# Last FFN's weights loaded early in 128-row chunks, V buffers shared, and a planner that prices waiting

## Chip, cores, metric

One core of a Trainium2 chip. The metric is the device time of one execution in microseconds (us). Executions of one kernel scatter by 4 to 20 us here, so kernels are compared by ratios of runs on the same chip. Profiles are single executions. In them PE is TensorE, PEld its weight loads, DVE VectorE, ACT ScalarE, POOL GpSimd, and SP SyncE, which issues the loads of weights (SPq is its queue). "issue" is a wait for nothing that the profile shows. Buffer numbers are left out, so W is both the Q and K weights and the small buffer of w1 and w3. A step is one segment of each layer at work, and a pair of an FFN is 256 of its 4608 hidden columns, gate and up.

## The reference, cut to what matters

```python
x = A_x                                    # 2048 x 576
x = x + _A_ref(_layernorm(x), ...)         # recurrent memory attention, 64 segments of 32 rows
x = x + _B_ref(_layernorm(x), ...)         # gated FFN, 576 -> 4608 -> 576
x = x + _A_ref(_layernorm(x), ...)         # the same weights again
x = x + _B_ref(_layernorm(x), ...)
# in _A_ref, for each segment s: h = [mem (8 rows), xs (32 rows)]; q, k, v = h Wq, h Wk, h Wv
# (32 heads of 128); o = softmax(q k / sqrt(128) + mask) v Wo; mem = o[:8]; out = o[8:]
```

The memory makes the 64 segments of one attention layer a chain. The kernel runs layer 2 eight segments behind layer 1: steps 0 to 7 have one layer, 8 to 63 two, 64 to 71 one. Every four steps a block of 128 rows is ready for an FFN, whose work fills TensorE between the parts of the chain. The last FFN, after step 71, has nothing beside it.

## The kernel before

A planner in Python simulates the engines and fixes the order of all work. On TensorE it takes, of the items that can start first, the one of lowest priority number plus a penalty if it needs another tiling mode (full, 64-row, 32-column, ...):

```python
if e == "PE":
    key = lambda x: x[1].prio + (mode_pen if x[1].mode != mode else 0.0)
...
pool_ = [x for x in ests if x[0] <= t + 1e-9]
pick = min(pool_, key=key)
```

V products of a segment come in two pieces (one in one-layer steps), each with its own buffer; a tail of 64 rows in another mode follows each piece:

```python
for k in ((0,) if one else (0, 1)):
    sl = Slot(f"vx{k}", users=4 if one else 2)
    m_ = node("PE", 8 * 0.2165, em.vx(t, k, b, False),
              deps=deps + [vx_pe.get(k), vx_pe.get(1) if one else None], ..., mode="c32", acq=[sl] + b)
    n = vx_pe[k] = node("PE", 0.2165, em.vx(t, k, b, True), deps=[m_], ..., mode="oct")
```

The FFNs stream their weights through small buffers. The last one loads them, in nine chunks, over the attention weights (W for Q and K, WV, WO), when all that reads the last segment is done, in halves of 64 rows:

```python
tail = [load("tail", kb(128, 9 * 512 + 4 * 576), s0 + 0.01 * i, em.tail_load(i),
             deps=reads_ht[nst - 1] + ([yx[1, nseg - 1]] if i == 8 else [])) for i in range(9)]
...
for r, wd in ((0, self.a.w1), (R64, self.a.w3)):      # tail_load
    self.dma(t13[r:r + R64], wd[:, fa:fa + 512].rearrange("(c p) f -> p c f", p=R64))
...
for fb in range(2):                                    # ffn_up: 36 matmuls of 64 rows per pair
    for c in range(NCH):
        for r in (0, 1):
            rr = slice(r * R64, (r + 1) * R64)
            self.mm(self.bk(b[r])[...], W[rr, c, fb * P:(fb + 1) * P], self.T.XTB[rr, POS[c], lo:hi], ...)
```

## Time and profile before

| | before |
|---|---|
| median | 2974.65 us (2973.45 to 2979.82, 4 runs) |
| TensorE busy | 96% |
| from the rows of step 63 to those of step 70 (one-layer steps) | 235.7 us |
| from the rows of step 70 to the last instruction | 109.8 us |

"The rows of step k" is, here and below, the moment at which ScalarE starts to copy step k's memory rows from PSUM into HT; it ends one step of the chain, and the timeline shows it. The prediction shows the main lines. Three further rows of the busy times by stretch (start:end, length, busy of PE, PEld, DVE, ACT, POOL with instructions, clock, DMA share, GB/s) cut the end as the result needs it:

```profile
2631.40:2867.10 235.70, 228.83 (x6248) 188.36 (x6245) 169.37 (x419) 88.62 (x255) 4.24 (x7) 1.00 0.54 124
2867.10:2908.60 41.50, 30.57 (x824) 24.59 (x816) 20.19 (x53) 11.40 (x34) 0.58 (x1) 0.90 0.72 158
2908.60:2976.90 68.30, 41.22 (x731) 33.13 (x730) 25.10 (x60) 10.48 (x24) 1.15 (x2) 0.75 0.91 180
```

One-layer steps with PE busy 97%; step 71, 41.5 us; the last FFN and the store, 68.3 us with PE busy 60% and DMA at 0.91.

### The profile page before, as it was taken

How to read it: one execution, taken by the hardware profiler on the slowest of the kernel's cores; microseconds unless marked ns; L12 is line 12 of the kernel's file. 1: busy time of each engine (PE TensorE's matmuls, PEld its weight loads, DVE VectorE, ACT ScalarE, POOL GpSimd, SP SyncE). 2: the span in 40 equal slices, each digit the busy share in tenths (PEclk: the TensorE clock that was granted, in tenths of full speed). 3: DMA queues.
4: the chain of work that ended last, by engine and by line, in shares of the span. 5: the costliest groups of instructions: out<-in, count | busy, mean ns of one | idle time of the engine just before them, and what ended most of it. 6: DMA issues, size and time to landing. Idle time of an engine off the chain costs nothing.

```text
span 2976.9 us, 147413 instructions
## 1 busy us (share of the span) xinstructions
PE 2866.2 (96%) x68021; PEld 2342.9 (79%) x68021; DVE 2068.5 (69%) x5015; ACT 1078.2 (36%) x2684; POOL 63.7 (2%) x108
## 2 busy tenths in 40 slices
PE   5999999999999999999999999999999999999985
PEld 4777878788888888888888888888888888888874
DVE  3566677776767777776777677677867777677753
ACT  1343333333334333343434333333433334333431
POOL 0000000000000000000000000000000000000000
PEclk7999999999999999999999999999999999999997
DMA  9065544444444444435344543444444444545479
GB/s 291 4 134 121 118 105 105 100 96 98 98 106 99 98 97 105 103 88 114 90 103 92 116 100 90 99 104 98 97 99 104 100 98 93 117 101 122 114 156 185
DMA packets 483275, 324.46 MB, mean 109 GB/s; under 512 B 16600, under 2 KB 477792, under 8 KB 482656
## 3 DMA queue, kind: packets, MB, share of 16 engines
q1 hardware_dynamic: 479584, 307.96, 45.9%
q8 instruction: 531, 8.70, 1.3%
q0 software_dynamic: 3072, 7.08, 0.8%
q14 instruction: 88, 0.72, 0.1%
HBM read 310.26 MB, written 2.36 MB: 105 GB/s over the span
## 4 chain that ended last, share of the span: by engine, by line
PE 90%; issue 3%; DMA 3%; DVE 2%; ACT 1%; SPq 1%; POOLq 0%; POOL 0%; DVEq 0%; ACTq 0%
PE bank L478 70%; PE YB L478 13%; PE SB L478 7%; DMA W<-in_B_w_dram 1%; DMA W<-in_A_Wk_dram 1%; ACT HT L481 1%; SPq L487 1%; DVE QKT L484 1%; DVE SME L484 0%; DVE STAT L484 0%; ACT QKT L481 0%; DVE PB L484 0%; DVE HT L484 0%; DVE HTT L484 0%; ACT XTB L481 0%
## 5 line engine op out<-in xcount | busy, mean ns | idle before, releaser
L478 PEld LDWEIGHTS <-W 128*128 128x128 bf16 (+1 forms) x34632 | 1241.4, 97 | 163.3 <-issue 71.2
L478 PE MATMUL bank<-HT,W 128*128 128x80 bf16 (+3 forms) x23040 | 807.6, 197 | 13.9 <-issue 5.5
L478 PE MATMUL bank<-XTB,W 64*128 64x256 bf16 (+1 forms) x11592 | 621.4, 260 | 21.4 <-DMA W<-in_B_w_dram 10.9
L481 ACT ACTIVATE QKT<-bank 128x320 bf16<-128x320 f32 (+1 forms) x801 | 279.7, 408 | 591.7 <-PE bank L478 589.2
L478 PE MATMUL bank<-WV,HT 128*32 128x512 bf16 (+3 forms) x8000 | 457.8, 386 | 11.2 <-DMA WV<-in_A_Wv_dram 5.4
L478 PE MATMUL YB<-OT,WO 128*128 128x80 bf16 (+1 forms) x11520 | 436.4, 197 | 15.3 <-issue 8.2
L478 PEld LDWEIGHTS <-WO 128*128 128x128 bf16 x11520 | 411.2, 99 | 44.1 <-issue 32.4
L481 ACT ACTIVATE HTT<-bank 128x512 bf16<-128x512 f32 (+1 forms) x324 | 178.1, 550 | 434.9 <-PE bank L478 432.7
L478 PEld LDWEIGHTS <-HT 128*32 128x32 bf16 (+3 forms) x8000 | 174.2, 93 | 201.7 <-issue 53.8
L484 DVE TENSOR_TENSOR PB<-SME,STAT 40x256 bf16<-40x256 f32 (+1 forms) x1024 | 320.4, 318 | 17.2
L478 PE MATMUL bank<-W2C,HTT 128*128 128x288 bf16 x2232 | 321.8, 287 | 0.6 <-DVE HTT L484 0.2
L484 DVE TENSOR_REDUCE STAT<-SME 104x8 f32<-104x320 f32 (+1 forms) x576 | 276.9, 481 | 55.8 <-ACT SME L481 48.7
L484 DVE SCALAR_TENSOR_TENSOR XR<-bank,XR 128x288 f32<-128x288 f32 x576 | 246.9, 450 | 68.6 <-PE bank L478 61.7
L484 DVE SCALAR_TENSOR_TENSOR HTT<-HTT,bank 128x512 bf16<-128x512 bf16 (+1 forms) x324 | 202.1, 624 | 126.1 <-ACT HTT L481 122.0
L478 PEld LDWEIGHTS <-HTT 128*128 128x128 bf16 x2304 | 205.1, 98 | 61.8 <-DVE HTT L484 7.2
L481 ACT ACTIVATE OT<-bank 128x320 bf16<-128x320 f32 (+1 forms) x356 | 137.5, 408 | 298.9 <-PE bank L478 294.3
L484 DVE CAST QKT<-bank 128x320 bf16<-128x320 f32 (+1 forms) x351 | 144.3, 446 | 145.9 <-PE bank L478 145.2
L484 DVE TENSOR_TENSOR HTT<-HTT,bank 128x512 bf16<-128x512 bf16 (+1 forms) x324 | 203.6, 628 | 24.5 <-DVE HTT L484 0.5
L484 DVE TENSOR_TENSOR SME<-SB,maskb 104x320 f32<-104x320 f32 (+1 forms) x288 | 136.8, 475 | 85.1 <-PE SB L478 81.2
L484 DVE CAST VX<-bank 128x512 bf16<-128x512 f32 x127 | 83.8, 686 | 156.4 <-PE bank L478 156.3
L481 ACT ACTIVATE SME<-SME 104x320 f32<-104x320 f32 (+1 forms) x288 | 135.2, 469 | 152.9 <-DVE SME L484 152.2
L484 DVE CAST OT<-bank 128x320 bf16<-128x320 f32 (+1 forms) x220 | 97.8, 446 | 109.1 <-PE bank L478 107.1
(63 smaller groups left out, 1922.0 us busy)
## 6 DMA issues: line engine op xcount, KB each, us to landing
W<-in_B_w_dram SPq DMA_DIRECT2D x612, 288.0 KB, 4.9
W2C<-in_B_w_dram SPq DMA_DIRECT2D x306, 288.0 KB, 4.0
W<-in_B_w_dram SPq DMA_DIRECT2D x16, 576.0 KB, 15.2
XR<-in_A_x_dram POOLq DMA_DIRECT2D x16, 288.0 KB, 3.0
WO<-in_A_Wo_dram SPq DMA_DIRECT2D x4, 1152.0 KB, 8.6
WV<-in_B_w_dram SPq DMA_DIRECT2D x8, 576.0 KB, 15.5
W<-in_A_Wq_dram SPq DMA_DIRECT2D x8, 512.0 KB, 8.1
W<-in_A_Wk_dram SPq DMA_DIRECT2D x8, 512.0 KB, 9.1
```

Source lines behind the costliest of these rows:

```text
L478: self.ch("PE", self.nc.tensor.matmul(out, lhsT=lhsT, rhs=rhs, start=start, stop=stop, skip_group_check=True, **k))
L481: self.ch("ACT", self.nc.scalar.activation(*a, **k))
L484: self.ch("DVE", getattr(self.nc.vector, fn_)(*a, **k))
L487: self.ch("SP", self.nc.sync.dma_start(out=out, in_=in_))
```

## The change

Its intent: the loads for the last FFN start as soon as the weights that they overwrite are dead (V weights after the last V product, then W, then WO); 128-row chunks; job 16, the last but one FFN, spreads over 3.0 steps for 3.64; V buffers go to whichever piece is next, and each piece waits for the tail of the piece before it (the chain); the planner looks 16 ns ahead, prices waiting, and gives a bonus to modes with much ready work; the priorities are tuned anew. Cut to its core:

```diff
-        key = lambda x: x[1].prio + (mode_pen if x[1].mode != mode else 0.0)
+        pool_ = [x for x in ests if x[0] <= t + o.hor]
+        work = {}
+        for x in pool_:
+            work[x[1].mode] = work.get(x[1].mode, 0.0) + x[1].dur
+        key = lambda x: (x[1].prio + o.wait * (x[0] - t)
+                         + (o.mode_pen - o.bulk * min(work[x[1].mode], 4.0) if x[1].mode != mode else 0.0))
...
-    qk, qkt, sc, ... = 0.0372, -0.0358, 0.0268, ...        # 15 of 17 priorities differ
+    qk, qkt, sc, ... = 0.0079, -0.0342, 0.0268, ...
+    ... hor, wait, bulk, ff_split, last_win, tail_at = ..., 0.0162, 0.141, 0.02, False, 3.0, -1.5
...
-            sl = Slot(f"vx{k}", users=4 if one else 2)
+            sl = Slot("vx", users=4 if one else 2)
-            m_ = node(..., deps=deps + [vx_pe.get(k), vx_pe.get(1) if one else None], ...)
-            n = vx_pe[k] = node(...)
+            m_ = node(..., deps=deps + [vx_pe.get(0)], ...)
+            n = ... = vx_pe[0] = node(...)
...
+        if t == nst - 1:                     # step 71: V of the memory rows first
+            m_.prio = n.prio = t
+            last_reads[0].extend([m_, n])
...
-            tail = [load(..., deps=reads_ht[nst - 1] + ...) for i in range(9)]
+                    parts = [(None, 9 * 512 + 4 * 576, v_done if i < 2 else qk_done if i < 8 else o_done)]
+                tail.append([load("tail", ..., s0 + o.tail_at + 0.01 * i, em.tail_load(i, what), deps=dep) ...])
-                prio = s0 + o.ff + o.win * pr_ / NPR
+                prio = s0 + o.ff + (o.win if s0 + 4 < nst else o.last_win) * pr_ / NPR
...
+                for kind, wd in ((0, self.a.w1), (1, self.a.w3)):          # tail_load, 128 rows
+                    self.dma(t13[:, 4 * kind:4 * kind + 4], wd[0:4 * P, fa:fa + 512].rearrange("(c p) f -> p c f", p=P))
+                if tail is False:                                          # ffn_up: 16 full + 4 half
+                    for r in (0, 1):
+                        for c in range(4):
+                            self.mm(self.bk(b[r])[:, os_], W[:, 4 * r + c, fs], self.T.XTB[:, c, lo:hi], ...)
```

More of the change, by code (lines that the diff above doesn't have):

```diff
@@ L37 @@
 POS = [c // 2 if c % 2 == 0 else 4 + c // 2 for c in range(NCH - 1)] + [8]
-POOLS = {"bank": 6, "s": 1, "y": 1, "qkt": 4, "vx0": 1, "vx1": 1, "vm": 1, "sme": 2, "pb0": 1, "pb1": 1, "pts": 1, "ot": 1,
+POOLS = {"bank": 6, "s": 1, "y": 1, "qkt": 4, "vx": 2, "vm": 1, "sme": 2, "pb0": 1, "pb1": 1, "pts": 1, "ot": 1,
          "xr": 4, "xn": 2, "w13": 2, "w2": 3, "htt": 4}
@@ L65, in after, with plan @@
         self.left = len(self.deps)
-def plan(nodes, pools, mode_pen=0.12, hold=0.0):
+def plan(nodes, pools, o):
     for n in nodes:
@@ L114, in plan @@
         if e == "PE":
-            key = lambda x: x[1].prio + (mode_pen if x[1].mode != mode else 0.0)
+            pool_ = [x for x in ests if x[0] <= t + o.hor]
[4 more added lines that the diff above has]
+                             + (o.mode_pen - o.bulk * min(work[x[1].mode], 4.0) if x[1].mode != mode else 0.0))
         else:
+            pool_ = [x for x in ests if x[0] <= t + 1e-9]
             key = lambda x: x[1].prio
-        pool_ = [x for x in ests if x[0] <= t + 1e-9]
-        pick = min(pool_, key=key)
-        if e == "PE" and hold:
-            late = [x for x in ests if x[0] <= t + hold and key(x) + 0.3 < key(pick)]
-            if late:
-                pick = min(late, key=key)
-        st, n = pick
+        st, n = min(pool_, key=key)
         dur = n.dur
@@ L148, in plan @@
                 free[s.pool][s.i] = s.end
-        for o in n.outs:
+        for o_ in n.outs:
             lat = n.lat
-            if o.eng == e == "PE":
+            if o_.eng == e == "PE":
                 lat = 0.0
-            o.ready = max(o.ready, n.end + lat)
-            o.left -= 1
-            if o.left == 0:
-                push(o)
+            o_.ready = max(o_.ready, n.end + lat)
+            o_.left -= 1
+            if o_.left == 0:
+                push(o_)
         order.append(n)
@@ L184 @@
 class Opt:
-    qk, qkt, sc, tr, pv, wo, wog = 0.0372, -0.0358, 0.0268, 0.0346, 0.0, 0.3, 0.049
-    vm, vmt, vx, vxt = 0.1, 0.0813, 0.55, 0.102
-    ff, fft, win, w2 = 0.2124, -0.05, 3.6429, -0.0064
-    gstep, ustep = 0.005, 0.02
-    mode_pen, hold = 0.12, 0.0
-    ff_split = False
+    qk, qkt, sc, tr, pv, wo, wog, vm = 0.0079, -0.0342, 0.0268, 0.1447, 0.0406, 0.2653, 0.0725, 0.1407
+    vmt, vx, vxt, ff, fft, win, w2, gstep = -0.0231, 0.2313, 0.0843, 0.2124, -0.1839, 3.5294, 0.1943, 0.0624
+    ustep, mode_pen, hor, wait, bulk, ff_split, last_win, tail_at = 0.0315, 0.1194, 0.0162, 0.141, 0.02, False, 3.0, -1.5
 def make_nodes(em, nseg, pools, o=Opt, dma_bw=230e3, load_bw=340e3):
@@ L238, in make_nodes @@
     ht_mem = {t: [] for t in range(nst + 1)}
+    steps = [{} for _ in range(nst)]
     def ln_nodes(tag, src, xn, deps, prio, wr, cost, wdeps):
@@ L256, in make_nodes, with vx_node @@
     vx_slots, vx_nodes, vx_pe = {}, {}, {}
-    def vx_node(t, prio):
+    def vx_node(t, prio, step_):
         ls = layers_of(t)
@@ L265, in vx_node @@
         for k in ((0,) if one else (0, 1)):
-            sl = Slot(f"vx{k}", users=4 if one else 2)
+            sl = Slot("vx", users=4 if one else 2)
             b = banks()
-            m_ = node("PE", 8 * 0.2165, em.vx(t, k, b, False), deps=deps + [vx_pe.get(k), vx_pe.get(1) if one else None],
+            m_ = node("PE", 8 * 0.2165, em.vx(t, k, b, False), deps=deps + [vx_pe.get(0)],
                       prio=prio + 0.01 * k, mode="c32", acq=[sl] + b, name="VX")
-            n = vx_pe[k] = node("PE", 0.2165, em.vx(t, k, b, True), deps=[m_], prio=prio + 0.01 * k + o.vxt, mode="oct", name="VXt")
+            step_[f"VX{k}"] = m_
+            n = step_[f"VXt{k}"] = vx_pe[0] = node("PE", 0.2165, em.vx(t, k, b, True), deps=[m_], prio=prio + 0.01 * k + o.vxt, mode="oct", name="VXt")
             reads_ht.setdefault(t, []).extend([m_, n])
-            ev = [node("AD", ew(512), em.vx_ev(t, k, r, b[r]), deps=[n], prio=prio, rel=[b[r]], name="VXe") for r in (0, 1)]
+            ev = [node("AD", ew(512), em.vx_ev(sl, r, b[r]), deps=[n], prio=prio, rel=[b[r]], name="VXe") for r in (0, 1)]
             for kk in ((0, 1) if one else (k,)):
@@ L284, in step @@
         if t == 0:
-            vx_node(0, 0.12)
+            vx_node(0, 0.12, steps[0].setdefault("first", {}))
         vm = Slot("vm", users=4)
@@ L292, in step @@
         rd += [m_, n]
+        me = steps[t]
+        me["VM"], me["VMt"] = m_, n
+        if t == nst - 1:
+            m_.prio = n.prio = t
+            last_reads[0].extend([m_, n])
         vme = [node("AD", ew(512), em.vm_ev(t, r, b[r]), deps=[n], prio=t + o.vm, rel=[b[r]], name="VMe") for r in (0, 1)]
@@ L306, in step @@
                 rd += [m_, n]
+                me[f"QK{u}"], me[f"QKt{u}"] = m_, n
                 for kind in (0, 1):
@@ L326, in step @@
             ot = Slot("ot")
-            pv = node("PE", 8 * mm80, em.pv(t, g, pts, b), deps=[pe_] + vme + vx_nodes[t, k], prio=pf + o.pv,
+            pv = node("PE", 8 * mm80, em.pv(t, g, pts, vx_slots[t, k], b), deps=[pe_] + vme + vx_nodes[t, k], prio=pf + o.pv,
                       mode="row", acq=b + [ot], rel=[pts, vm, vx_slots[t, k]], name="PV")
@@ L334, in step @@
             wos.append(wo)
+            me[f"SC{g}"], me[f"TR{g}"], me[f"PV{g}"], me[f"WO{g}"] = sc, tr, pv, wo
+        if t == nst - 1:
+            last_reads[1].extend(me[f"QKt{u}"] for u in range(8))
+            last_reads[2].extend(wos[:2])
         nxt = [li for li in ls if t - LAG * li + 1 < nseg]
@@ L355, in make_nodes @@
     last_up = [None]
+    last_reads = [], [], []
     def job(j):
@@ L368, in job @@
         prev_ff = last_up[0]
-        cost = ewh(512, 128, 128) if o.ff_split else ewh(512, 640, 512, 640)
+        split = last or o.ff_split
+        cost = ewh(512, 128, 128) if split else ewh(512, 640, 512, 640)
         for (bi, g) in ents:
             pa = post(bi, g)
-            wr.append(ln_nodes("F", xr[g], Slot("xn"), [pa], s0, (lambda bi=bi: lambda b: em.xtb_write(bi, b))(), cost, [prev_ff]))
+            wr.append(ln_nodes("F", xr[g], Slot("xn"), [pa], s0, (lambda bi=bi: lambda b: em.xtb_write(bi, b, split))(), cost, [prev_ff]))
         mm = (128 * ne / 2.4 + 2.5) / 1000
@@ L376, in job @@
         if last:
-            tail = [load("tail", kb(128, 9 * 512 + 4 * 576), s0 + 0.01 * i, em.tail_load(i),
-                         deps=reads_ht[nst - 1] + ([yx[1, nseg - 1]] if i == 8 else [])) for i in range(9)]
+            v_done, qk_done, o_done = last_reads
+            tail = []
+            for i in range(9):
+                if i == 2:
+                    parts = [(0, 9 * 512, v_done), (1, 4 * 576, qk_done)]
+                else:
+                    parts = [(None, 9 * 512 + 4 * 576, v_done if i < 2 else qk_done if i < 8 else o_done)]
+                tail.append([load("tail", kb(128, c), s0 + o.tail_at + 0.01 * i, em.tail_load(i, what), deps=dep) for what, c, dep in parts])
         for pp in range(NPR // 2):
@@ L381, in job @@
             for pr_ in (2 * pp, 2 * pp + 1):
-                prio = s0 + o.ff + o.win * pr_ / NPR
+                prio = s0 + o.ff + (o.win if s0 + 4 < nst else o.last_win) * pr_ / NPR
                 if last:
                     w13 = w2 = None
-                    ld = [tail[pp]]
+                    ld = tail[pp]
                 else:
@@ L393, in job @@
                 rel13 = [w13] if w13 else []
-                if o.ff_split:
+                if split:
                     fm = node("PE", 16 * mm, em.ffn_up(ents, pr_, w13, b, last, False), deps=wr + ld, prio=prio, mode="full",
@@ L449, in make_nodes @@
         if t + 1 < nst:
-            vx_node(t + 1, t + o.vx)
+            vx_node(t + 1, t + o.vx, steps[t])
     return nodes
@@ L562, in load_w2, with tail_load @@
         return lambda n: self.dma(self.T.W2C[:, w2.i], self.a.w2[fa:fa + 2 * P, :].rearrange("(b p) d -> p b d", p=P))
-    def tail_load(self, i):
+    def tail_load(self, i, what):
         def f(n):
@@ L568, in f @@
             qk, wv, wo = T.W[:].rearrange("p a b -> p (a b)"), T.WV[:], T.WO[:].rearrange("p a b -> p (a b)")
-            n13, n2 = NCH * 512, 4 * D
-            t13 = qk[:, i * n13:(i + 1) * n13] if i < 8 else wv[:, 0:n13]
-            t2 = wv[:, n13 + i * n2:n13 + (i + 1) * n2] if i < 6 else wo[:, (i - 6) * n2:(i - 5) * n2]
+            n13, n2 = 9 * 512, 4 * D
+            k = n13 + n2
+            if i < 2:
+                t13, t2 = wv[:, i * k:i * k + n13], wv[:, i * k + n13:(i + 1) * k]
+            elif i == 2:
+                t13, t2 = wv[:, 2 * k:2 * k + n13], qk[:, 5 * k:5 * k + n2]
+            elif i < 8:
+                t13, t2 = qk[:, (i - 3) * k:(i - 3) * k + n13], qk[:, (i - 3) * k + n13:(i - 2) * k]
+            else:
+                t13, t2 = wo[:, 0:n13], wo[:, n13:k]
             fa = i * 512
-            t13 = t13.rearrange("p (c f) -> p c f", c=NCH)
-            for r, wd in ((0, self.a.w1), (R64, self.a.w3)):
-                self.dma(t13[r:r + R64], wd[:, fa:fa + 512].rearrange("(c p) f -> p c f", p=R64))
+            t13 = t13.rearrange("p (c f) -> p c f", c=9)
             t2 = t2.rearrange("p (b d) -> p b d", b=4)
-            self.dma(t2, self.a.w2[fa:fa + 512, :].rearrange("(b p) d -> p b d", p=P))
+            if what != 1:
+                for kind, wd in ((0, self.a.w1), (1, self.a.w3)):
+                    self.dma(t13[:, 4 * kind:4 * kind + 4], wd[0:4 * P, fa:fa + 512].rearrange("(c p) f -> p c f", p=P))
+                for kind, wd in ((0, self.a.w1), (1, self.a.w3)):
+                    self.dma(t13[kind * R64:(kind + 1) * R64, 8], wd[4 * P:D, fa:fa + 512])
+            if what != 0:
+                self.dma(t2, self.a.w2[fa:fa + 512, :].rearrange("(b p) d -> p b d", p=P))
             for h in range(2):
@@ L658, in ht_write, with xtb_write @@
         return f
-    def xtb_write(self, bi, b):
+    def xtb_write(self, bi, b, split):
         def f(n):
             ps = self.lnps(b)
+            dst = self.T.XTB[:, :, bi * P:(bi + 1) * P]
+            if split:
+                self.cp(n, dst[:, 0:4, :], ps[:, 0:4, :])
             for r in (0, R64):
-                dst = self.T.XTB[r:r + R64, :, bi * P:(bi + 1) * P]
-                self.cp(n, dst[:, 0:4, :], ps[0:R64, 0:4, :])
-                self.cp(n, dst[:, 4:NCH, :], ps[R64:P, 0:5, :])
+                if split:
+                    self.cp(n, dst[r:r + R64, 4, :], ps[R64:P, 4, :])
+                else:
+                    self.cp(n, dst[r:r + R64, 0:4, :], ps[0:R64, 0:4, :])
+                    self.cp(n, dst[r:r + R64, 4:NCH, :], ps[R64:P, 0:5, :])
         return f
@@ L694, in vx, with vx_ev @@
         return f
-    def vx_ev(self, t, k, r, b):
-        return lambda n: self.cp(n, self.T.VX[:, k, r, :], self.bk(b)[:])
+    def vx_ev(self, vx, r, b):
+        return lambda n: self.cp(n, self.T.VX[:, vx.i, r, :], self.bk(b)[:])
     def vm(self, t, b, tail):
@@ L828, in pt_ev, with pv @@
         return f
-    def pv(self, t, g, pts, b):
+    def pv(self, t, g, pts, vx, b):
         def f(n):
@@ L834, in f @@
             r, k = g // 2, g % 2
-            vk = k if len(ls) == 2 else 0
             PT = self.T.PTS[:, pts.i, 0:GH * nq].rearrange("p (m h q) -> p m h q", m=2, h=4)
             for hl in range(4):
-                for m, V in ((0, self.T.VX[:, vk, r]), (1, self.T.VM[:, r])):
+                for m, V in ((0, self.T.VX[:, vx.i, r]), (1, self.T.VM[:, r])):
                     for ab in (0, 1):
@@ L906, in span, with ffn_up @@
         return min(bis) * P, (max(bis) + 1) * P
-    def ffn_up(self, ents, pr, w13, b, last):
+    def ffn_up(self, ents, pr, w13, b, last, tail=None):
         def f(n):
@@ L912, in f @@
             for fb in range(2):
-                for c in range(NCH):
+                fs = slice(fb * P, (fb + 1) * P)
+                os_ = slice(fb * 2 * P + lo, fb * 2 * P + hi)
+                if tail is False:
+                    for r in (0, 1):
+                        for c in range(4):
+                            self.mm(self.bk(b[r])[:, os_], W[:, 4 * r + c, fs], self.T.XTB[:, c, lo:hi], fb == 0 and c == 0, False)
+                    continue
+                for c in ((8,) if tail else range(NCH)):
                     for r in (0, 1):
                         rr = slice(r * R64, (r + 1) * R64)
-                        self.mm(self.bk(b[r])[:, fb * 2 * P + lo:fb * 2 * P + hi], W[rr, c, fb * P:(fb + 1) * P],
-                                self.T.XTB[rr, POS[c], lo:hi], c == 0, c == NCH - 1, tile_position=(r * R64, 0))
+                        self.mm(self.bk(b[r])[:, os_], W[rr, c, fs], self.T.XTB[rr, 4 if tail else POS[c], lo:hi],
+                                c == 0, c == NCH - 1, tile_position=(r * R64, 0))
         return f
@@ L1016 @@
     T.QKT = sp.tile([P, pools["qkt"], 2, 4, 2 * QW], BF, name="QKT")
-    T.VX = sp.tile([P, 2, 2, 512], BF, name="VX")
+    T.VX = sp.tile([P, pools["vx"], 2, 512], BF, name="VX")
     T.VM = sp.tile([P, 2, 512], BF, name="VM")
@@ L1050 @@
         nc.vector.memset(b[:], 0.0)
-    order, _ = plan(nodes, pools, Opt.mode_pen, Opt.hold)
+    order, _ = plan(nodes, pools, Opt)
     for n in order:
```

## The prediction

> **What bounds the kernel now.** I read the page first: busy shares, the slices, the chain that ended last.
>
> ```profile
> span 2976.9 us, 147413 instructions
> PE 2866.2 (96%) x68021; PEld 2342.9 (79%) x68021; DVE 2068.5 (69%) x5015; ACT 1078.2 (36%) x2684; POOL 63.7 (2%) x108
> ...
> PE   5999999999999999999999999999999999999985
> ...
> DMA  9065544444444444435344543444444444545479
> ...
> PE 90%; issue 3%; DMA 3%; DVE 2%; ACT 1%; SPq 1%; POOLq 0%; POOL 0%; DVEq 0%; ACTq 0%
> ```
>
> TensorE is full from the second slice to the third last; DMA is full only in the first and the last. So there are two regimes, and I cut the span accordingly. Stretches: eight steps of the two-layer body, then the last recurrence step (71) before and after its last V product, the last FFN, the end. The step limits are the copies of the memory rows from PSUM into HT (67.1, 95.6, ... 2834.5, 2867.1 us).
>
> ```profile
> 1011.10:1352.60 341.50, 339.26 (x7726) 277.35 (x7725) 247.65 (x589) 127.04 (x303) 7.62 (x12) 1.00 0.45 100
> 2867.10:2889.10 22.00, 18.40 (x497) 13.98 (x490) 12.27 (x32) 7.07 (x23) 0.00 (x0) 0.92 0.37 86
> 2889.10:2913.20 24.10, 12.89 (x341) 11.06 (x337) 10.43 (x28) 4.64 (x12) 1.15 (x2) 0.80 1.12 238
> 2913.20:2965.00 51.80, 35.50 (x648) 28.49 (x650) 19.98 (x48) 8.73 (x20) 0.00 (x0) 0.80 1.09 213
> ```
>
> Columns: stretch, length, busy time of PE, PEld, DVE, ACT, POOL, clock, DMA share, GB/s. In the body PE is busy 339.3 of 341.5 us at full clock and DMA at 0.45: only less PE work can shorten it. From 2889 on DMA stands at 1.1 (full) with 213 to 238 GB/s, and PE is busy only 48 of 76 us at a clock of 0.80.
>
> The tail loads are 9 chunks of 128 x (4608 + 2304) x 2 B = 1.77 MB, 15.9 MB in all. The issue rows show them starting at about 2889: all nine were declared to wait for every reader of HT in step 71, and the last V products end at 2887.4. At 213 GB/s 15.9 MB take 75 us, 2889 to 2964; the last group of up-products starts at 2965.0, and 12 us later all is over. The end is thus a DMA-bound stretch that begins 22 us after step 71 does. The timeline of those stretches shows a second sign:
>
> ```profile
> 2895.28 0.58 PE L478 MATMUL YB<-OT,WO 128*128 128x40 bf16 x17 [0.32 <-DVE OT L484]
> ...
> 2899.64 0.24 PE L478 MATMUL YB<-OT,WO 128*128 128x40 bf16 x3 [3.78 <-issue]
> ...
> 2929.83 2.63 PE L478 MATMUL bank<-XTB,W 64*128 64x128 bf16 x61 [2.46 <-issue]
> ...
> 2956.78 4.02 PE L478 MATMUL bank<-XTB,W 64*128 64x128 bf16 x71 [3.06 <-DMA W<-in_B_w_dram]
> ```
>
> PE stops inside one group of 40 matmuls with every operand there, for 3.78 us, named "issue": it has no instruction to run. The page gives 531 packets and 8.70 MB for instructions, 16 KB each. In the trace those packets start at 2897.1, 2905.8, 2913.8, 2927.1, 2936.3, 2945.2, 2954.0: mostly 8 to 9 us apart (13 at one place), and PE resumes about 2.5 us after each. In the body they come every 4 to 8 us and PE hardly waits (8.1 + 2.4 + 1.9 us of "issue" in the waits of PE between 64 and 2867 us).
>
> **What the Trainium skill says.** (1) "Runtime: NRT & Kernel Launch", Instruction fetch mechanics: instructions come in blocks of 16 KiB, 256 instructions, by a DMA queue of their own, and the cost is mostly hidden. The size agrees (8.70 MB over 531 packets); hidden is right for the body and wrong beside a full DMA, where the trace has stalls of 1.9 to 3.8 us. A matmul is two instructions (68021 MATMUL and as many LDWEIGHTS), so a block is 128 matmuls. (2) "TensorEngine Tiling (Array Packing)", Tiling Modes, Key Properties: "Changing tiling mode (not just tile) drains the TensorE". The trace agrees: inside a run of 128-row matmuls of 80 columns the starts are 36 ns apart, at a change of mode from such a run 130 to 134 ns, so about 96 ns each. (3) "DMA: Bandwidth & Descriptors", Rules for kernel authors: two transfers to disjoint partition halves gain nothing, one transfer over 128 partitions is to be used. The tail loads come in halves of 64 rows and reach 213 to 238 GB/s; the loads of the first 60 us, over 128 rows for the most part, reach 325 GB/s, though of other tensors, some with longer rows. (4) "TensorE: Matmul & The Clock Gate", Part 1: idle lowers the clock. Granted 1.00 in the body, 0.80 in the tail: agrees.
>
> **The change, part by part.**
>
> *Early tail loads.* Chunks 0, 1 and the up-weights of 2 go into the V weights, free after step 71's VM product, which also gets the first priority of that step. It has 32 + 8 matmuls (1.9 + 0.4 us in the timeline), so they can start at about 2867 + 4 = 2871, not 2889. That is 4.7 MB, 16 to 20 us at 240 to 300 GB/s, just about what the Q and K products then need to set W free for the next five chunks. So the loads run from 2871 almost without a hole: 15.9 MB at an estimated 260 GB/s (between 213 and 325) take 61 us, to 2932; at the old 213 they would take 75, to 2946.
>
> *128-row chunks.* A pair of up-products takes 16 + 4 matmuls for 36. PE time stays: 36 half-height ones ran in 1.18 us, two at a time; 16 of 56 ns (the pitch of the 128-column transposes) and 4 of about 30 ns, with two mode changes of 0.1, are 1.2 us. Instructions do not stay: the FFN goes from 18 x 36 + 72 = 720 matmuls (5.6 blocks) to 18 x 20 + 72 = 432 (3.4 blocks). At 8.8 us per block with DMA full that is 50 us (the FFN took 51.8) against 30. The copies into XTB before it (four, 2.64 us of ACT and waits of PE to 2916.7) become three smaller ones: -1.5 us.
>
> *Last windows.* Job 16 spreads over 3.0 steps, not 3.64: by 68.21 + 3.64 x pr / 18 > 71 pairs 14 to 17 fell into step 71 (the timeline shows four groups of 36 there), by 3.0 only pair 17 does. Three pairs with half a W2 group each, 3 x 1.9 = 6 us, move to steps 68 to 70; step 71 sheds as much.
>
> *Sum of the end.* Step 71 starts at 2867 + 6 = 2873. It keeps 616 + some 50 matmuls, 5.2 blocks; one runs free, four meet a full DMA at 8.8: about 41 us, no shorter than today's 41.5, for the stalls come earlier. Then layer norm 4.5 us, XTB 2, FFN 30, last adds and store 9: 2873 + 86.5 = 2959.5. The DMA path ends earlier (about 2877 to 2951 with the shifted start, then 9) and does not bind by itself. So the end gives about -17 us; with fewer stalls than assumed up to -28. I take -22.
>
> *Shared V buffers.* There are still two, and with two layers each step uses two, in the same order of release: nothing. With one layer a step used one, and V of the next step had to wait for the last PV (2864.0: the V product, 1.9 us, sits before the last WO and delays the memory rows). Now it fills another gap: about 0.5 us in each of some 10 such steps, -5 us. Against it, the second V piece now waits for the tail of the first, which can add two mode changes per step.
>
> *Planner.* It may wait 16 ns for a better item, hardly a hold; the real change is the bonus for modes with much ready work and re-tuned priorities. In the eight steps I count 218 changes of mode, 27 per step, 20.9 of 341.5 us. That is all it can win from. Scores (32 runs) and V products and tails (20 and 18) are fixed by their chain; of the 148 changes into the other two modes I guess 10 to 15 go, and V takes some back: -13 in eight steps, -1.25 us, times 7 for 56 steps: -9 us, and -1 for the rest.
>
> Total: -22 - 5 - 10 = -37 us; 2975 - 37 = 2938.
>
> **Rivals.** (a) *Early loads starve the instruction fetch*: DMA full for 25 us more during step 71, which is the critical chain. For: 3.78 and 2.56 us stalls as soon as DMA filled. If each block of step 71 costs 10 us (2886.4 to 2897.1 did), the end gains only 8 us: 2952. (b) *The search found a much better order*: 20 changes per step for 27 would be 0.67 us x 56 = 38 us; with the end -22 and -5 that is 2910. For: the pattern repeats every eight steps, so one better order counts seven times. Against: the order before was tuned in the same way, and PE never idles in it. (c) *Worse body*: the second V piece's new wait adds up to 2 changes per step, 56 x 0.2 = 11 us, and nothing else improves: 2958. (d) *DMA still binds the end*: the rate stays at 213 and SP, in order, holds tail loads behind a load that waits for a buffer; the end gains some 12 us: 2948.
>
> **Range and chances.** The rivals span 2910 to 2958. Range 2905 to 2960. Faster by 2% needs 2915.3, that is (b) together with a good end: 0.16. Within 2%: 0.82. Slower: 0.02, for no part adds work that PE must do.
>
> **What would show it.** Right: first load from a B weight into WV at about 4 us into step 71; FFN with 128-row matmuls, DMA falling off before it ends, "issue" waits inside step 71; the eight-step period at 339 to 341 us with 200 to 215 changes. Wrong: a period below 337 (planner under-rated) or above 342; tail loads still ending within 15 us of the last instruction; step 71 longer than 46 us.

## The result

2959.88 us median (2952.79 to 2963.62, 4 runs) against 2974.65: ratio 0.9944, interval 0.9922 to 0.9967. A gain of 15 us where 37 were forecast, at the very edge of the range. Measured again later, beside its own parts on another chip, the same kernel gave 0.9921 (0.9899 to 0.9943), so some 15 to 24 us. The page of the changed kernel:

```profile
span 2959.4 us, 146757 instructions
PE 2870.1 (97%) x67733; PEld 2328.3 (79%) x67733; DVE 2060.5 (70%) x4939; ACT 1150.1 (39%) x2759; POOL 63.6 (2%) x108
...
PE   5899999999999999999999999999999999999987
...
DMA  9055544434443433444343443434344344434567
...
PE 91%; DMA 3%; issue 2%; DVE 2%; ACT 1%; SPq 1%; POOL 0%; POOLq 0%; DVEq 0%; ACTq 0%
```

DMA no longer fills the last slices, and PE nearly does. The 288 matmuls fewer are the 18 x 16 of the last FFN. By stretch, as before:

```profile
1015.90:1356.20 340.30, 339.66 (x7726) 275.45 (x7724) 246.22 (x578) 137.41 (x315) 7.63 (x12) 1.00 0.41 100
...
2628.70:2877.80 249.10, 237.07 (x6330) 193.10 (x6327) 172.74 (x424) 92.44 (x261) 4.24 (x7) 0.98 0.53 121
2877.80:2913.60 35.80, 26.51 (x736) 22.66 (x735) 17.28 (x45) 10.36 (x34) 0.58 (x1) 0.81 1.04 299
2913.60:2959.40 45.80, 34.46 (x442) 26.96 (x442) 25.93 (x60) 9.04 (x23) 1.15 (x2) 0.84 0.51 153
```

Eight steps of the body: 340.3 for 341.5. Steps 64 to 70: 249.1 for 235.7. Step 71: 35.8 for 41.5, now with DMA full. The last FFN: 45.8 for 68.3, DMA half idle. The whole account by the rows of step 12, 63 and 70: +0.2, -2.9, +13.3, -28.2, together -17.5 us, the difference of the two spans. The last FFN in the timeline of TensorE:

```profile
2932.87 1.14 PE L498 MATMUL bank<-W,HTT 128*128 128x288 bf16 x8
2933.95 2.50 PE L498 MATMUL bank<-XTB,W 64*128 64x128 bf16 x40
2936.28 1.14 PE L498 MATMUL bank<-W,HTT 128*128 128x288 bf16 x8
2937.36 2.50 PE L498 MATMUL bank<-XTB,W 64*128 64x128 bf16 x40
```

Two pairs of up-products (40 matmuls, the row counts the 64-row form, 32 of them have 128 rows) and one group of down-products every 3.41 us, with no wait: TensorE sets the pace of the FFN now. The waits of PE from the rows of step 70 on (us in total, times, longest), before and after:

```profile
PE bank L478 <- issue: 7.5, 5, 2.5
PE YB L478 <- issue: 6.3, 2, 3.8
PE bank L478 <- DMA W<-in_B_w_dram: 6.2, 4, 3.1
PE bank L478 <- DMA WV<-in_B_w_dram: 1.7, 1, 1.7
```

```profile
PE bank L498 <- issue: 2.8, 1, 2.8
PE SB L498 <- issue: 2.4, 2, 1.5
PE bank L498 <- DMA W<-in_B_w_dram: 1.3, 1, 1.3
```

The 7.9 us of waits for loads and 4.3 of the 13.8 us named "issue" stood in the last FFN; after the change none of either does. Earlier loads, fewer instructions and 128-row transfers can all have a part in that, and they were not run apart. So the end gained more than forecast, and the shortfall lies elsewhere. In the body, between the rows of steps 12 and 63, the waits of PE tell what the new order does; the main ones first of the kernel before, then of the changed one:

```profile
PE SB L478 <- DVE QKT L484: 6.5, 25, 0.3
PE bank L478 <- ACT HT L481: 2.4, 4, 0.6
```

```profile
PE bank L498 <- ACT HT L501: 2.4, 4, 0.6
PE bank L498 <- issue: 0.5, 1, 0.5
```

The scores no longer wait for their Q and K copies, and the time in which PE is not busy falls from 11.6 to 3.4 us in that stretch. But changes of tiling mode, counted by walking the matmuls in order of start, rise from 218 to 238 in eight steps. At the 96 ns of the prediction that is 1.9 us more per eight steps. As the eight steps shown still got 1.2 us shorter, some 3.1 us of waiting went, by this estimate. Of it 1.6 us stands as idle time of PE (2.24 us in the row of the prediction, 0.64 in the row above); where the rest lies is not shown. So, by the estimate, the mode changes ate more than half of what the waits gave. Over a longer stretch, steps 16 to 56, the mean period is 340.38 for 341.08.

### The profile page after: what moved, and what is told of

It reads as the page before. It is cut to its first block, busy times and chain, and to the rows that moved or that the text cites. A ratio compares the mean times of both kernels' runs of the same rounds, so it can differ in the third digit from the quotient of the medians.

```text
span 2959.4 us, 146757 instructions
## 1 busy us (share of the span) xinstructions
PE 2870.1 (97%) x67733; PEld 2328.3 (79%) x67733; DVE 2060.5 (70%) x4939; ACT 1150.1 (39%) x2759; POOL 63.6 (2%) x108
## 4 chain that ended last, share of the span: by engine, by line
PE 91%; DMA 3%; issue 2%; DVE 2%; ACT 1%; SPq 1%; POOL 0%; POOLq 0%; DVEq 0%; ACTq 0%
PE bank L498 71%; PE YB L498 12%; PE SB L498 7%; DMA W<-in_B_w_dram 1%; DMA W<-in_A_Wk_dram 1%; ACT HT L501 1%; SPq L507 1%; DVE SME L504 0%; DVE STAT L504 0%; DVE HTT L504 0%; DVE PB L504 0%; DMA W2C<-in_B_w_dram 0%; DVE XR L504 0%; DVE LNS L504 0%; ACT XTB L501 0%
## 5 line engine op out<-in xcount | busy, mean ns | idle before, releaser
L498 PE MATMUL bank<-HT,W 128*128 128x80 bf16 (+2 forms) x23040 | 815.4, 197 | 8.9 <-issue 2.5
L498 PE MATMUL bank<-XTB,W 64*128 64x256 bf16 (+2 forms) x11216 | 619.6, 260 | 15.4 <-DMA W<-in_B_w_dram 9.7
L498 PE MATMUL bank<-WV,HT 128*32 128x512 bf16 (+3 forms) x8000 | 468.6, 387 | 12.2 <-DMA WV<-in_A_Wv_dram 5.7
L501 ACT ACTIVATE QKT<-bank 128x320 bf16<-128x320 f32 (+1 forms) x694 | 249.8, 405 | 487.4 <-PE bank L498 485.4
L504 DVE CAST QKT<-bank 128x320 bf16<-128x320 f32 (+1 forms) x458 | 198.7, 453 | 170.7 <-PE bank L498 170.2
L498 PE MATMUL bank<-W2C,HTT 128*128 128x288 bf16 x2232 | 315.2, 287 | 0.5
L504 DVE SCALAR_TENSOR_TENSOR XR<-bank,XR 128x288 f32<-128x288 f32 x576 | 248.4, 453 | 75.0 <-PE bank L498 65.0
L501 ACT ACTIVATE OT<-bank 128x320 bf16<-128x320 f32 (+1 forms) x394 | 149.5, 408 | 240.8 <-PE bank L498 240.2
L501 ACT ACTIVATE PTS<-SB 128x640 bf16<-128x640 bf16 (+1 forms) x250 | 162.2, 649 | 185.8 <-PE SB L498 185.3
```

The lines of the kernel that those rows point to most:

```text
L498: self.ch("PE", self.nc.tensor.matmul(out, lhsT=lhsT, rhs=rhs, start=start, stop=stop, skip_group_check=True, **k))
L501: self.ch("ACT", self.nc.scalar.activation(*a, **k))
L504: self.ch("DVE", getattr(self.nc.vector, fn_)(*a, **k))
```

## The experiments

In all of them outputs were correct. The "tail part" is the early loads, the 128-row chunks and V first in step 71, together. "Window" is the spread of job 16 in steps, "old plan" the old rule with the old priorities, "new plan" the new ones. Step lengths are from each run's profile.

| run | tail part | window | plan | V buffers | ratio to before | rows 12 to 63 | rows 63 to 70 | rows of 70 to end |
|---|---|---|---|---|---|---|---|---|
| before | no | 3.64 | old | separate | 1 | 2168.9 | 235.7 | 109.8 |
| after | yes | 3.0 | new | shared, chained | 0.9944 | 2166.0 | 249.0 | 81.6 |
| e1 | yes | 3.64 | old | separate | 0.9984 | 2168.7 | 236.4 | 108.7 |
| e2 | yes | 3.0 | old | separate | 0.9919 | 2168.3 | 244.8 | 80.5 |
| e3 | yes | 3.0 | new priorities, old rule | shared, chained | 0.9994 | 2176.6 | 249.7 | 77.8 |
| e4 | yes | 3.53 | new | shared, chained | 0.9931 | 2167.1 | 246.2 | 86.8 |
| e5 | yes | 3.0 | new | separate | 0.9963 | 2167.1 | 253.8 | 79.3 |
| e6 | yes | 3.0 | old | shared, chained | 0.9967 | 2178.2 | 244.4 | 81.9 |
| e7 | yes | 3.0 | new in steps 8 to 63 only | shared, chained | 0.9925 | 2167.0 | 242.9 | 79.3 |
| e8 | yes, gap filled | 3.0 | old | separate | 0.9936 | 2169.5 | 244.6 | 77.6 |
| f1 | yes | 3.0 | old | separate | 0.9933 | 2167.7 | 243.1 | 82.3 |
| f2 | yes | 3.0 | old | shared, chained | 0.9951 | 2177.1 | 243.1 | 78.2 |
| f3 | yes | 3.0 | new | separate | 0.9955 | 2166.4 | 254.3 | 76.9 |
| f4 | yes | 3.0 | new | shared, chained | 0.9921 | 2165.5 | 244.1 | 81.2 |
| g1 | yes | 3.0 | old | shared, not chained | 0.9936 | 2168.7 | 245.0 | 78.7 |
| g2 | yes | 3.0 | new | shared, not chained | 0.9915 | 2166.3 | 246.8 | 81.7 |
| g3 | yes, gap filled | 3.0 | new | shared, chained | 0.9927 | 2166.4 | 248.4 | 78.1 |
| g4 | yes, gap filled, last chunks late | 3.0 | new | shared, chained | 0.9923 | 2165.9 | 248.8 | 78.5 |

The runs e1 to e4, e5 to e8, f1 to f4 and g1 to g4 shared a chip each; intervals are about 0.0013 to 0.0022 to either side. Ratios of different groups differ by about as much.

### e1: the tail part alone

```diff
 # the kernel before, with the new tail_load, ffn_up, xtb_write, V first in step 71; and
+    ... last_win, tail_at = 3.6429, -1.5
```

> The kernel before with the tail part alone: early loads, 128-row chunks, V product first in step 71; V buffers, planner rule, priorities and the last window (3.6429) as before. Theory A (the end is worth about 28 us after the memory rows of step 70, the rest of the change nets +13): body and one-layer steps as before, memory rows of step 63 at 2631 us and of step 70 at 2867 +- 2, then 82 to 86 us: 2950 +- 4 us, thus faster than the whole change (2960). Rival B (the early loads stand ahead of job 16's own loads in SP's order, and its last four pairs then wait): step 71 has waits on W from B's weights and gets longer than 45 us, total 2962 to 2972.

Ratio 0.9984 (0.9965 to 1.0002), 2977.72 us: no gain. Rival B. One of the waits of PE from the rows of step 70 on, and the loads in SP's own timeline:

```profile
PE bank L498 <- DMA W<-in_B_w_dram: 26.3, 2, 25.8
```

```profile
2892.66 25.83 SPq L507 DMA_DIRECT2D W<-in_B_w_dram  x26
2918.59 5.33 SPq L507 DMA_DIRECT2D WO<-in_B_w_dram  x5
2923.98 2.46 SPq L507 DMA_DIRECT2D W<-in_B_w_dram  x2
2926.48 1.75 SPq L507 DMA_DIRECT2D W2C<-in_B_w_dram  x1
```

The last two lines are the loads of job 16's last pair. They stand behind the 31 tail loads of the lines above, in the one queue, and TensorE waits 25.8 us for them before the last FFN can begin. B had put the wait into step 71; it fell after it (step 71 took 39.0 us). The total is what B said: by the ratio, 2970 us on the first chip. With the old window the tail part alone is worth nothing.

### e2: the same with the window at 3.0

```diff
-    ... last_win = 3.6429
+    ... last_win = 3.0
```

> As the run with the tail part alone, with the last window 3.0 instead of 3.6429. If B holds, this frees job 16's loads: 2950 +- 5 and 10 us or more faster than with 3.6429. If A holds, the window only shifts three pairs from step 71 to steps 68 to 70: within 4 us of the tail part alone.

Ratio 0.9919 (0.9900 to 0.9938), 2957.64 us, 20 us faster than e1 on the same chip: as B said (by the ratio 2951 on the first chip). The window costs 8.4 us in steps 64 to 70 (244.8 for 236.4) and gives 28.2 in the end (80.5 for 108.7). With the plan and the V buffers untouched, this has the whole gain of the change.

### e3: the old rule with the new priorities

```diff
-    ... mode_pen, hor, wait, bulk = 0.1194, 0.0162, 0.141, 0.02
+    ... mode_pen, hor, wait, bulk = 0.1194, 1e-9, 0.0, 0.0
```

> The changed kernel with the planner's old rule (no look ahead, no price on waiting, no bonus for bulk) and all its new priorities. Theory C (the rule buys off short waits with more mode changes; it is what shortens the eight-step period from 341.5 to 340.3): changes of mode fall from 238 to about 200 in eight steps, waits and in-run gaps grow, the period is 344 to 347, total 2980 to 2995. Rival D (the new priorities do it, the rule is idle): period 340 +- 1, total 2960 +- 5. Rival E (my prediction's: fewer changes are better): faster than 2955.

Ratio 0.9994. Theory C in direction, not in size: the period rose to 342.5, not to 344 to 347. Mode changes fell to 192 in eight steps, the fewest that I counted, and steps 12 to 63 took 10.6 us longer than with the rule (the steps up to 12 another 14). Its main waits between the rows of steps 12 and 63:

```profile
PE bank L498 <- ACT QKT L501: 18.1, 77, 0.2
PE bank L498 <- DMA W<-in_B_w_dram: 1.1, 3, 0.6
```

77 waits of about 0.23 us for a copy of Q or K. My prediction's idea, that the new plan gains by fewer mode changes (rival E), is refuted: the new rule makes more changes, and pays with them for not waiting. The run turns off the look ahead, the price on waiting and the bonus at once, so which of the three does it, and what the bonus alone does, is not shown.

### e4: the window back at 3.5294

```diff
-    ... last_win = 3.0
+    ... last_win = 3.5294
```

> The changed kernel with the last window back at 3.5294. Rival F (the window of 3.0 is what makes steps 63 to 70 13 us longer): memory rows of step 70 6 us or more earlier than 2878 and step 71 longer by as much or less; total 2950 to 2957 if step 71 hides them. Theory G (half-clock spells and fetch stalls do it): rows of step 70 within 3 us of 2875, total 2958 to 2970, since the four pairs then wait in step 71 behind the early loads.

0.9931, 2962.58 us. Rows of step 63 to 70: 246.2 (249.0 in the changed kernel), end 86.8 (81.6). F's 6 us did not come back: the rows of step 70 came at 2875.2 us, where G had them. G's wait came too: from there on TensorE waits 7.1 us for W from B's weights (two times, longest 5.9), with loads of job 16 again behind early loads in SP's queue. It is less than the 26.3 us of e1; as this window is 3.53 and not 3.64, whether that is due to the plan or to the window is open. The total tells nothing: 2962.58 us is in G's range, but by the ratio it is 2954 on the first chip, in F's.

### e5 and e6: V buffers, under each plan

```diff
 # e5: the changed kernel
-            sl = Slot("vx", ...);       deps + [vx_pe.get(0)]
+            sl = Slot(f"vx{k}", ...);   deps + [vx_pe.get(k), vx_pe.get(1) if one else None]
 # e6: e2 with the reverse
```

> The changed kernel with one V buffer for each piece again, and with the pieces no longer chained (each waits only for its own piece of the step before). Theory H (sharing is worth little; the two pieces' chain costs mode changes but no time): within 4 us of the changed kernel, 2956 to 2964, eight-step period 340 +- 1. Rival I (sharing is what spoils the first steps: memory rows of step 0 to step 8 take 245.1 us against 237.5): that stretch back at 238 +- 2 and total 2950 to 2955. Rival J (sharing is worth the 5 us that I predicted in the one-layer steps): total 2964 to 2970.

> The run with tail and window 3.0 alone, plus shared V buffers; old rule and old priorities. H: within 4 us of it (ratio 0.9919 to before). I: steps 0 to 8 rise from 235 to 242 or more and the ratio to 0.994 or more. J: ratio 0.990 or less.

e5 0.9963, e6 0.9967. Sharing, with its chain, helps under the new plan and hurts under the old, so none of H, I and J holds as put under both. Rival I's stretch from step 0 to step 8 was a wrong measure, too: in e5 it took 248.2 us and in before 237.5, but by the rows of step 12 they stand within 4.2 us of each other (before 462.5, after 462.7, e5 464.6, e6 460.4). FFN work only moves across the border.

### e7: the new plan only while both layers run

```diff
+    at = lambda t: Opt if 8 <= t < 64 else Old       # priorities and rule by step
```

> The changed kernel (tail, window 3.0, shared V), with the new priorities and the new rule only while both layers run (steps 8 to 63) and the old ones in the one-layer steps before and after. Theory K (the new plan gains 11.6 us in the body and loses it again in the one-layer steps): rows of step 0 to 8 in 235 to 240, of step 8 to 63 in 2315 +- 3, of step 63 to 70 in 241 to 246, end 81 +- 3: ratio 0.987 to 0.990, faster than either plan alone. Rival L (the one-layer loss comes with the body's order, by what it leaves undone at its borders): no faster than the tail and window alone, 0.992 or more.

0.9925, level with e2 (0.9919) and in L's range: K fell, though not by L's mechanism alone. Its 11.6 us had been measured from step 8, where FFN work still moves across the border; from step 12 to 63 the new order has 1.9 us to give (2167.0 for 2168.9).

### e8: useless matmuls in the gap of the last layer norm

```diff
+            if last:
+                node("PE", 8 * 0.2165, em.warm(8), deps=[pa.deps[0]], ...)   # 8 of 512 columns, into SB
```

> The run with tail and window 3.0 alone, plus eight matmuls of 512 columns without use, into a bank that is free by then, in the gap in which TensorE waits for the last layer norm. Theory M (the half clock over 24 to 32 us of the end is kept by idle TensorE, and costs half of the busy time in it): the half-clock time after the rows of step 70 falls from 31.8 us by 3 to 7, and the end shortens by 1.5 to 3.5 us. Rival N (idle does not matter, the clock comes back when the DMA load ends): no change in the half-clock time; the end the same or up to 1 us longer.

The end took 77.6 us for e2's 80.5, and the time at half clock after the rows of step 70 fell from 31.8 to 22.9 us. First e2, then e8, up to the first 76 up-products of the last FFN (nearly four pairs):

```profile
2914.71 6.77 PE L498 MATMUL bank<-XTB,WV 128*128 128x128 bf16 x76 [0.69 <-ACT XTB L501]
```

```profile
2913.39 3.26 PE L500 MATMUL SB<-VM,ident 128*128 128x512 bf16 x8
2917.07 0.45 PE L500 MATMUL bank<-ident,XN 128*128 128x128 bf16 x5 [0.42 <-DVE XN L506]
2918.21 4.71 PE L500 MATMUL bank<-XTB,WV 128*128 128x128 bf16 x76 [0.69 <-ACT XTB L503]
```

The same 76 matmuls in 4.71 for 6.77 us: M, with more half clock gone than its 3 to 7 us. Of the 8.9 us, 6.8 are of the one long spell (17.1 us for 23.9); the rest is at the very end. In e8, g3 and g4 this spell lasts 17.1 us, in the other runs with the tail part 20.5 to 27.3 (e1: 37.5). In the total (0.9936) it doesn't show; the first steps of that run happened to be 3 us longer.

### f1 to f4: two plans by two ways with V, on one chip

The kernels of e2, e6, e5 and after, five rounds.

> Two by two on one chip, all four with the tail part and window 3.0: old plan (rule and priorities), separate V. So far on other chips 0.9919. Theory P (new plan and shared V each shift some us, together they return part of what the tail gained): the lowest of the four or level with the changed kernel, 0.991 to 0.9935. Rival Q (the differences between chips made it look so): all four within 0.2% of each other, and the changed kernel not slower than this one.

> Old plan, shared V. P: 0.3% or more above the first (0.995 to 0.997), since the chained pieces add mode changes to an order not tuned for them (218 to 228 in eight steps). Q: within 0.1% of it.

> New plan, separate V (unchained). P: 0.995 to 0.997, since the new priorities were tuned for shared buffers. Q: within 0.1% of the first.

> New plan, shared V: the changed kernel itself, beside its parts. P: 0.993 to 0.995, slower than the first by 0.1 to 0.4%. Q: equal to the first or faster. If it is faster by 0.3% or more (0.989 or less against 0.992), then my prediction's -15 us for these two parts is right after all and the end is the mis-sized term.

0.9933, 0.9951, 0.9955, 0.9921. Either part alone is 0.2% slower than neither, about the size of one interval, and both groups of runs agree on it (e5, e6); both together are 0.12% below neither, well inside the intervals (0.9916 to 0.9951 and 0.9899 to 0.9943). P's claim that the whole change is slower than the tail alone did not hold, nor Q's that all four are level. Plan and V together are worth -3.6 us here (0.0012 x 2976); on the two chips of the first comparisons it was +7 (0.9944 less 0.9919). I call it 0, give or take 8 us (two intervals of about 0.002 add to 0.0028, or 8.4 us); the -15 of the prediction lies outside.

### g1 and g2: shared buffers without the chain

```diff
-            deps + [vx_pe.get(0)];   n = vx_pe[0] = node(...)
+            deps + [vx_pe.get(k), vx_pe.get(1) if one else None];   n = vx_pe[k] = node(...)
```

> Old plan, shared V buffers, but the second piece no longer waits for the tail of the first. Theory R (the chain is the cost): memory rows of step 12 to 63 back from 2177 to 2168 +- 2, mode changes in eight steps back from 228 to 218. Rival S (the shared buffers themselves upset the order): stays at 2175 or more.

> New plan, shared buffers, no chain. R: steps 12 to 63 at 2165 +- 2, as with the chain (the priorities were tuned with it), or a little less; mode changes 232 to 238 in eight steps. The one-layer steps 63 to 70 tell whether the 254 us of separate V come from the buffers (here 244 to 249) or from the missing chain (here 252 or more).

g1: steps 12 to 63 in 2168.7 for f2's 2177.1, mode changes in eight steps 218 for 228: theory R, the chain costs the old plan 8.4 us, the buffers nothing. g2: 2166.3, with 234 changes, and steps 63 to 70 in 246.8 where separate V has 254: there it is the shared buffers that save 7 us or so, chain or not.

### g3 and g4: the gap filled in the changed kernel, and the last chunks held back

```diff
+            # g3: em.warm(8) as in e8; g4 also:
-            v_done if i < 2 else qk_done if i < 8 else o_done
+            v_done if i < 2 else qk_done if i < 5 else qk_done + wo_done if i < 8 else o_done + wo_done
```

> The changed kernel plus eight useless 512-column matmuls in the gap of the last layer norm. M (idle keeps the clock at half): half-clock time after step 70's rows falls from 28 to 32 by 5 to 9, end (rows of step 70 to the last instruction) 77 to 80 against 81.4; ratio 0.1% lower than the changed kernel's.

> As the third, with chunks 5 to 8 held back until the last output products of step 71. Theory T (full DMA delays instruction fetch and so step 71): stalls named issue in step 71 shrink from about 5 to about 2 us and its length from 34 to 36 to 32 to 34 us; the last chunks still land in time (the last is needed about 27 us after the FFN starts; 4 chunks, 7.1 MB, take 22 to 28): end 75 to 78. Rival U (they now come late): the FFN waits on W and WO from B's weights and the end is 83 or more.

g3: half clock 21.7 us for 28.4 and 31.9, end 78.1 for 81.6 and 81.2, as M says; the ratio, 0.9927, doesn't show it. g4 changed nothing against g3: "issue" waits from the rows of step 70 on 4.4 for 4.5 us, end 78.5 for 78.1. DMA was as full as before (1.10 in the second half of step 71 in both), and SP took 28 us for the 26 loads into W with or without the hold. The hold never came to act: it is a dependency of the planner, which fixes the order of issue, and that order stayed the same. The first load of chunk 5 (the twelfth of the 26) is issued at 2908.4 us, while the last output products of step 71 run until 2913. T is untested, not refuted. No version is clearly faster than the changed kernel.

## Why the prediction was wrong

By its own steps:

- *What bounds the kernel*: right for the end, where TensorE waited for loads and for "issue". Wrong for the body, where "only less PE work can shorten it": the eight steps got 1.2 us shorter with PE busy for 339.66 instead of 339.26 us, and between the rows of steps 12 and 63 PE was busy for 2162.6 instead of 2157.3. What shrank is the waiting that I had taken for nothing.
- *Early loads and 128-row chunks*: right as far as seen, though the two were not run apart. The first load into WV is issued 6 us into step 71 (4 forecast), loads run at 299 to 331 GB/s where I had taken 260, step 71 takes 35.8 us (41 forecast), the FFN about 32 (30). From the rows of step 70 to the end, 81.6 us against 86.5.
- *Last window*: the mechanism was half seen. I took it as a shift of 6 us that step 71 gives back; it costs 8.4 (e1 to e2), and without it the whole end is lost to the order of one queue. I had that as rival (d), but put its cost at 10 us and did not see that the window is its cure.
- *The sum of the end*, -22: e2 and f1 give -24 and -20. Right, with some luck: the sum itself came to -17, and -22 was a choice, for fewer stalls than assumed. The waits named "issue" after the rows of step 70 did fall, from 13.8 to 5.2 us.
- *Planner, -10*, by "of the 148 changes into the other two modes I guess 10 to 15 go": **this failed.** 20 more came in eight steps (238 for 218). What it won was waits (PE not busy in steps 12 to 63: 3.4 for 11.6 us), most of it given back in mode changes; net -2.9 in that stretch. That the period of 340.3 us lies in the forecast 339 to 341 is luck: the count that was to bring it went the other way. So is that rival (c)'s 2958 is near the result, for the body did not get worse. e3, with fewer changes and 10.6 us more, shows that the count of changes was the wrong thing to sum.
- *Shared V buffers, -5*: no gain on top of the rest is shown. Under the new plan they save some 7 us in steps 63 to 70 against separate ones; but separate V under the old plan has 243 to 245 there already, as much as the changed kernel's 244 to 249. The buffers repair what the new priorities spoil. The chain I had named as a cost (two mode changes per step) is one of 8.4 us under the old plan and of nothing under the new, which comes with it.

So -22 stood, and of the -15 for plan and V some 0 is left. That the same kernel gained 15 us in one measurement and 24 in the other is scatter between runs: in its two profiles, 10.2 us at half clock between the rows of steps 63 and 70 in the one and 3.4 in the other, and 4.4 us between their rows of step 12. Of the +13.3 us between the rows of steps 63 and 70, some 8.4 are the window (e1 to e2). The nine runs with the new priorities in these steps have 3.4 to 10.2 us of half clock there; of the nine with the old ones only g1 has any (3.4).

How such a spell starts, from the timeline and the stretches of the changed kernel:

```profile
2899.66 0.19 PE L498 MATMUL bank<-PTS,VX 64*128 64x40 bf16 x2 [2.80 <-issue]
```

```profile
2900.00:2918.00 18.00, 10.32 (x245) 9.30 (x245) 8.80 (x23) 4.65 (x12) 1.15 (x2) 0.51 1.09 331
```

A stall of 2.80 us with DMA full, and from 2900.2 the trace's clock record has half the clock for 23.9 us; in the 18 us shown TensorE is busy 57% of the time. The order in time is the same in all 17 runs with the tail part: the long spell begins within a stall named "issue" of 0.97 to 2.88 us, or some 2 us after it at most. Short spells between the rows of steps 63 and 70 also follow waits for loads (2.12 us in e4, 1.36 in f4), so idle time seems to start a spell, whatever its reason; no run was made to test it. That filling idle time ends the spell earlier is shown (e8, g3). What a slower early load would save in step 71 stays open.

## What to carry to other kernels

An early load pays only if nothing that is needed sooner stands behind it in the same queue: move the consumer before it, and check with each part alone. A planner's new rule, priorities and buffers are one design: measured two by two, each alone can lose what both together merely keep. When TensorE is full, ask of a new order both how many waits it removes and how many mode changes it adds; counting only one of them got the mechanism backwards here.

## What the Trainium skill lacked or had wrong

- "Runtime: NRT & Kernel Launch", Instruction fetch mechanics, calls the cost of the next 16 KiB block mostly hidden. Beside a full DMA (share 1.0 to 1.1) it is not: TensorE stalled 1.9 to 3.8 us at a time before the change, up to 2.80 us after, and went on some 2.5 us after an instruction packet began. That the full DMA is the cause is not shown: before the change there is a stall of 2.10 us from 2878.2 on with a DMA share of 0.00, and it too ends 2.5 us after such a packet began.
- "DMA: Bandwidth & Descriptors", Rules for kernel authors, has the rule for disjoint partition halves without a figure for what it is worth. The last FFN's weights, rows of 1 KB in both forms, came at 213 to 238 GB/s in halves and at 331 GB/s over 128 rows, at the same DMA share of 1.09 to 1.12; the two forms were not run apart from the rest of the tail part.
- "TensorE: Matmul & The Clock Gate", Part 1, has the full clock return after one window of about 3.4 us of sustained work, but not how busy such a window must be. Here TensorE busy for 57% of 18 us did not bring it back in a spell of 23.9 us; the dense work of the last FFN did, 4.6 us after it began at 2919.5. Filling 3.26 us of the gap before it with matmuls took 6.8 us off such a spell.
- "TensorEngine Tiling (Array Packing)", Key Properties, says that a change of mode drains TensorE but not what it costs: about 96 ns each in this kernel (130 to 134 ns between starts at a change, 36 inside a run).
